# First expert of a fused attention and mixture-of-experts kernel: later issue of the loads of paired words, two pools for the converted weights, idle products moved ahead of the first gather

## The chip, the cores and the metric

One core of a Trainium2 chip runs the whole kernel as one program. The metric is the device time of that program in microseconds (us); less is better. Three runs of the kernel before gave 1026.57, 1030.37 and 1033.47 us; the median is 1030.37 us.

## The reference

The reference chains three parts. Causal attention with a learned position bias (4 batches, 8 heads, 576 tokens, 64 per head) gives a matrix x of 2304 tokens by 512. A first mixture of experts sends each token to one of 8 experts, 288 tokens to each, by a greedy assignment over sorted gate values, and applies two matrices with a ReLU between. A second block, the same for all tokens, applies `w_in` (512 by 2048), a mish-like function, and `w_out` (2048 by 512).

```
logits = x @ w_gate                      # greedy by value, 288 tokens to each expert
h = np.maximum(x[mask] @ w1[e], 0.0)     # e = 0..7, 512 -> 1024
out[mask] = h @ w2[e]                    # 1024 -> 512
...
h = x @ w_in                             # all tokens, 512 -> 2048
sp = np.log1p(np.exp(h))
return (h * np.tanh(sp)) @ w_out         # 2048 -> 512
```

## The kernel before, in words

**Split products.** All large products are made in a reduced-precision float type from split operands: each operand a has a high part (a copy rounded by ScalarE) and a low part (a minus the high part, by GpSimd for weights, by VectorE for activations). Every product is three matmuls (lines 497 to 499, `mm3`): high by high, high by low, low by high. A pass over one weight block is 12 matmuls of 128x288.

**Expert stages.** After attention, `experts` handles the experts one after the other. `route(e)` finds the 288 tokens of expert e (thresholds, counts, a list `idx`) and gathers their rows by three indirect DMAs issued by GpSimd (line 402, tile xg). `make_xt` turns the gathered rows by TensorE (line 531), ScalarE makes the high half (line 534) and VectorE the low half (line 535) of xu. `up(e)` runs the first mixture: for m = 0 to 7 a pass hp(m) = w1 block by xu, then act(m) (ScalarE line 558 for the high part, VectorE line 559 for the low part), and one step later a pass y(m-1) = w2 block by act(m-1). Its result goes to xu again (lines 578 and 579). `down(e)` runs the second block over 16 values of f: a pass with WI[f], the mish chain (lines 590 to 605), a pass with WO[f]. For expert 0, `route(0)` runs alone before `up(0)`; for the later ones route(e+1) is interleaved with up(e) and down(e).

**Weights.** Raw expert weights are loaded by SyncE's queue (line 458), copied to the high half by ScalarE (line 466), subtracted to the low half by GpSimd (line 467). In `up(0)` the sixteen blocks of the first expert are put into WI[8..15] and WO[8..15] (`home`), which `down(0)` needs later for the second block's own weights.

**Conversion of the second block's weights.** `w_in` and `w_out` come as 64-bit words that hold a double. The class `Convert` makes them into 32-bit floats and splits them, once, for all experts. Its units are 32 single ones (128x256) for WI[0..7], WO[0..7], and 16 paired ones (128x512) for WI[8..15], WO[8..15]. A unit is: a load into a buffer r2 (printed as r; three buffers, line 78; issued by ScalarE's queue in the expert stages), three VectorE operations (lines 115, 118, 121), then the split: a ScalarE copy (line 91) and a GpSimd subtraction (line 92). Some 21 single units are converted by VectorE during attention into the memory of xu, act and ot; they are held, and `settle` issues their splits during route(0). `run` is a generator: each `next` emits one VectorE operation (the third with the split), and the program calls it at fixed places (`conv`, `tick`). A paired unit may start only when `up(0)` has used the first expert's block in the same place (`gate`).

**What sets the order.** Every engine runs its instructions in the order in which the program emits them, and the order is the same in every run. ScalarE's queue carries its activations and also the loads of r2: an instruction that waits holds all that is behind it. In `run`, `fetch(i)` at the start of unit i issues the load of unit i+2. The buffer of that load was unit i-1's, so the load waits for the GpSimd subtraction of unit i-1.

**Pools.** All WI and WO tiles come from one pool, m_w, opened when attention's pools are closed; its memory is memory that attention's tiles used, and the first writers wait for the last users of those tiles, the stores of x to DRAM among them (lines 1075, 1078).

**Idle products.** `awake(n)` (line 679) issues n bf16 matmuls of 128x512 into a bank that nobody reads. Ahead of the first gather's data there are 18, and 4 more behind each third of `make_xt(0)`.

Of the kernel before, what the change touches and what calls it, by code (L numbers as in the profile page):

```python
# [30 lines left out]
def fb(ap):  # L31
    return ap.bitcast(F32)


class Convert:
# [25 lines left out]
        self.places = list(self.slots()) if self.wide else []  # L61
        self.limit = len(self.places)

    def grow(self, pool, stage, depth):
        for f in range(F2 // 128):
            self.WI.append(pool.tile([128, 2, DM // 128, 128], F32R, name=f"WI{f}"))
            self.WO.append(pool.tile([128, 2, DM], F32R, name=f"WO{f}"))
        self.limit, self.pool, self.depth, self.most = len(self.units), stage, depth, 4
# [10 lines left out]
        self.raw[self.loaded] = t  # L79
        self.loaded += 1  # L80

    def fetch(self, i):
        while self.loaded < min(self.limit, i + self.depth[0]):
            self.load()

    def split(self, unit, t):
# [11 lines left out]
    def run(self):  # L98
        nc = self.nc
        for i, unit in enumerate(self.units):  # L100
            while i >= min(self.limit, self.gate):
                yield
            self.fetch(i)
            t = self.raw.pop(i)
            keep = self.wide and i < len(self.places)
            if self.wide:
                w = t.bitcast(I32).rearrange("p c (f w) -> p c f w", w=2)
                if keep:
                    a = self.places[i]
                elif unit[3] == 1:  # L110
                    a = self.pool.tile([128, 2, 128], I32, name="c1", bufs=self.depth[1])
                else:
                    a = w[:, :, :, 1]
                b = a if self.temp is None else self.temp[:, :2 * unit[3]]
                nc.vector.tensor_scalar(b, w[:, :, :, 1], 3, 0x3FFFFFFF, op0=OP.logical_shift_left,
                                        op1=OP.bitwise_and)
                yield
                nc.vector.scalar_tensor_tensor(b, w[:, :, :, 1], -0x40000000, b, op0=OP.bitwise_and,
                                               op1=OP.bitwise_or)
                yield  # L120
                nc.vector.scalar_tensor_tensor(a, w[:, :, :, 0], 29, b, op0=OP.logical_shift_right,
                                               op1=OP.bitwise_or)
                t = fb(a)
                if keep:
                    self.held.append((unit, t))
            if not keep:
                self.split(unit, t)
            self.done += unit[3]
            yield
# [52 lines left out]
def build(ctx, tc, q, k, v, s, w_gate, w1, w2, w_in, w_out, out, debug=None):  # L182
# [29 lines left out]
    with ExitStack() as mctx:  # L212
        experts(mctx, tc, K, ring, ident, L, x_dram, w1, w2, cv, out)


def experts(ctx, tc, K, ring, ident, L, x_dram, w1, w2, cv, out):
    nc = tc.nc
    NF1, NF2, NC, NJ, JW = F // 128, F2 // 128, DM // 128, 3, CAP // 3
    rot = ctx.enter_context(tc.tile_pool(name="m_rot", bufs=2))
    one = ctx.enter_context(tc.tile_pool(name="m_one", bufs=1))  # L220
    W = ctx.enter_context(tc.tile_pool(name="m_w", bufs=1))
    ps_h = ctx.enter_context(tc.tile_pool(name="ps_h", bufs=1, space=PSUM))
    ps_y = ctx.enter_context(tc.tile_pool(name="ps_y", bufs=4, space=PSUM))
    ps_r = ctx.enter_context(tc.tile_pool(name="ps_r", bufs=1, space=PSUM))

    cv.grow(W, rot, (3, 4))
    cv.queue = nc.scalar
# [20 lines left out]
    def hbank():  # L248
        if cv.done == 4 * NF2 and len(free) == 2:
            free.insert(0, words)  # L250
        free.append(free.pop(0))
        return free[-1]
# [234 lines left out]
    def conv(n):  # L487
        for _ in range(n):
            next(cv.steps, None)
# [34 lines left out]
    def make_xt(e, parts=range(NJ), between=0):  # L524
        for j in parts:
            if j == 0:
                XT[e] = ring("xu", [128, 2, NC, CAP], F32R)
            xg, xt = R[e, "xg"][j], XT[e]
            p = hbank()
            for c in range(NC):  # L530
                nc.tensor.transpose(p[:, JW * c:JW * c + JW], xg[:JW, 128 * c:128 * c + 128], ident[:JW, :JW])
            src = p[:, :NC * JW].rearrange("p (c t) -> p c t", c=NC)
            js = slice(JW * j, JW * j + JW)
            nc.scalar.activation(xt[:, 0, :, js], src, AF.Copy)
            nc.vector.tensor_sub(xt[:, 1, :, js], src, fb(xt)[:, 0, :, js])  # L535
            if between:
                awake(between)
# [139 lines left out]
    def awake(n, at=None):  # L677
        for _ in range(n):
            nc.tensor.matmul(idle if at is None else at, upper, upper[:, None, :].to_broadcast([128, 4, 128]),
                             start=True, stop=True)  # L680
# [12 lines left out]
    cv.settle(99)  # L693
    rows(bank)
    conv(8)
    awake(18)
    make_xt(0, range(NJ), 4)
    conv(4)
    feed()
    for e in range(E):  # L700
# [503 lines left out]
```

## Time and profile before

| | us |
|---|---|
| median of three runs (lowest, highest) | 1030.37 (1026.57, 1033.47) |
| the profiled execution | 1027.31 |
| its span, first to last instruction | 1025.6 |
| mean granted TensorE clock, share of full speed | 0.984 |
| TensorE matmul busy | 957.2 (93%) |
| ScalarE busy | 631.8 (62%) |
| VectorE busy | 607.1 (59%) |
| GpSimd busy | 462.1 (45%) |

All rows below come from the one profiled execution. PE is TensorE's matmul, PEld its weight load, DVE VectorE, ACT ScalarE, POOL GpSimd, SP SyncE; ACTq is ScalarE's queue while it issues a DMA. In a timeline row the first number is the start in us from the start of the span, the second the duration in us; brackets hold the idle time of that engine just before and what ended it. Which instruction ended it is inferred, and where an engine stood behind a DMA in its own queue the name given can be another's. Attention ends at about 283 us, route(0) at 310, up(0) runs from 315 to 357, down(0) to 428, and the other seven experts take about 85 us each.

### The profile page before, as it was taken

What the parts mean: (1) busy time and instruction counts of PE and PEld (TensorE: products, weight loads), DVE (VectorE), ACT (ScalarE), POOL (GpSimd) and SP (SyncE); (2) the same over time, 40 slices, a digit from 0 to 9 for tenths busy, and PEclk for the clock granted to TensorE, in tenths of its full rate; (3) what the DMA queues carried; (4) which work ended last, traced back from release to release, by engine and by line L of the source; (5) the groups of instructions that cost most, each with busy time, mean ns of one, the idle gap of its engine ahead of it and who ended that gap; (6) DMA issues with size and microseconds to landing.
All of it is one profiled execution on the core that took longest, in us unless ns stands there. A gap on an engine that the chain in (4) does not pass through costs nothing.

```text
span 1025.6 us, 21405 instructions
## 1 busy us (share of the span) xinstructions
PE 957.2 (93%) x7679; PEld 901.2 (88%) x7679; DVE 607.1 (59%) x1871; ACT 631.8 (62%) x1403; POOL 462.1 (45%) x485
## 2 busy tenths in 40 slices
PE   5889998999988689899999999999999999999996
PEld 4779887888847588899999999999999999999996
DVE  6877898898586668446445544643644554343342
ACT  7668766777844366536745745663674575675563
POOL 2888888787677623360260343126026024502401
PEclk8999999999999899999999999999999999999998
DMA  5677686763147423231231121213123122401200
GB/s 123 159 173 169 162 213 158 177 163 88 44 141 246 130 66 114 65 95 47 61 106 42 56 76 41 66 53 96 42 66 106 36 62 77 135 12 38 69 1 24
DMA packets 131058, 97.31 MB, mean 95 GB/s; under 512 B 63272, under 2 KB 113608, under 8 KB 130920
## 3 DMA queue, kind: packets, MB, share of 16 engines
q1 hardware_dynamic: 120280, 75.24, 28.3%
q10 hardware_dynamic: 7600, 11.27, 3.5%
q0 software_dynamic: 3072, 9.44, 3.0%
q8 instruction: 60, 0.98, 0.4%
q14 instruction: 46, 0.38, 0.1%
HBM read 69.55 MB, written 9.73 MB: 77 GB/s over the span
## 4 chain that ended last, share of the span: by engine, by line
PE 60%; DVE 14%; issue 13%; ACT 6%; POOL 5%; DMA 1%; ACTq 0%; SPq 0%; POOLq 0%; DVEq 0%
PE y L497 8%; PE y L498 7%; PE y L499 7%; PE hp L497 5%; PE hp L498 5%; PE hp L499 5%; PE words L497 3%; PE words L499 2%; PE words L498 2%; PE rt L298 2%; PE t L935 2%; PE pv L1042 1%; PE pv L1040 1%; DVE junk L941 1%; PE s L1005 1%
## 5 line engine op out<-in xcount | busy, mean ns | idle before, releaser
L467 POOL TENSOR_TENSOR wt<-raw,wt 128x512 fp32r<-128x512 f32 x112 | 142.9, 1290 | 194.3 <-ACT wt L466 193.8
L497 PE MATMUL y<-act,WO 128*128 128x288 f32 x516 | 155.4, 301 | 3.3 <-ACT act L558 3.3
L1020 POOL TENSOR_TENSOR Pl<-P,Ph 128x384 fp32r<-128x384 f32 (+2 forms) x128 | 136.8, 1080 | 45.3 <-DVE Ph L1019 23.4
L498 PE MATMUL y<-act,WO 128*128 128x288 f32 x516 | 154.0, 298 | 0.2
L499 PE MATMUL y<-act,WO 128*128 128x288 f32 x516 | 153.0, 296 | 0.0
L497 PE MATMUL hp<-xu,WI 128*128 128x288 f32 x372 | 114.6, 308 | 6.7 <-DVE c L599 2.9
L498 PE MATMUL hp<-xu,WI 128*128 128x288 f32 x372 | 110.5, 297 | 0.2 <-DVE xu L535 0.2
L499 PE MATMUL hp<-xu,WI 128*128 128x288 f32 x372 | 110.1, 296 | 0.0
L497 PEld LDWEIGHTS y<-act,WO 128*128 128x128 f32 x516 | 98.0, 190 | 3.6 <-ACT act L558 3.5
L498 PEld LDWEIGHTS y<-act,WO 128*128 128x128 f32 x516 | 97.9, 190 | 0.8 <-DVE act L605 0.6
L499 PEld LDWEIGHTS y<-act,WO 128*128 128x128 f32 x516 | 97.7, 189 | 0.0
L402 POOL DMA_INDIRECT xg<-x_dram,idx x24 | 22.5, 939 | 162.2 <-DVE rt L408 156.8
L466 ACT ACTIVATE wt<-raw 128x512 fp32r<-128x512 f32 x112 | 70.0, 625 | 41.5 <-PE y L499 21.8
L599 DVE SCALAR_TENSOR_TENSOR hp<-c,hp 128x288 f32<-128x288 f32 x75 | 34.5, 460 | 87.8 <-ACT c L594 87.8
L591 ACT ACTIVATE c<-c 128x288 f32<-128x288 f32 x128 | 56.4, 440 | 44.9 <-DVE c L590 41.8
L1012 ACT ACTIVATE P<-s 128x384 f32<-128x384 f32 (+2 forms) x128 | 63.3, 503 | 30.2 <-PE s L1005 18.6
L497 PEld LDWEIGHTS hp<-xu,WI 128*128 128x128 f32 x372 | 70.9, 190 | 10.6 <-DVE c L599 4.5
L1040 PE MATMUL pv<-Ph,VH 128*128 128x320 f32 (+4 forms) x224 | 71.1, 318 | 3.5 <-DVE xT L1059 3.5
L498 PEld LDWEIGHTS hp<-xu,WI 128*128 128x128 f32 x372 | 70.7, 190 | 0.7 <-DVE xu L535 0.4
L499 PEld LDWEIGHTS hp<-xu,WI 128*128 128x128 f32 x372 | 70.7, 190 | 0.0
L1003 PE MATMUL s<-QKB 128*128 128x320 f32 (+4 forms) x224 | 69.4, 310 | 0.8 <-DVE mx L941 0.8
L497 PE MATMUL y<-act,wt 128*128 128x288 f32 x224 | 69.1, 309 | 0.0
(288 smaller groups left out, 2962.8 us busy)
## 6 DMA issues: line engine op xcount, KB each, us to landing
raw<-in_moe_w_dram SPq DMA_DIRECT2D x120, 256.0 KB
QKB<-qk SPq DMA_DIRECT2D x55, 288.0 KB
qkraw<-in_q_dram SPq DMA_DIRECT2D x32, 128.0 KB
qkraw<-in_k_dram SPq DMA_DIRECT2D x32, 128.0 KB
vraw<-in_v_dram SPq DMA_DIRECT2D x32, 128.0 KB
x_dram<-xn SPq DMA_DIRECT2D x16, 256.0 KB
r<-in_moe_w_in_dram ACTq DMA_DIRECT2D x8, 512.0 KB
r<-in_moe_w_out_dram ACTq DMA_DIRECT2D x8, 512.0 KB
```

Source lines behind the costliest of these rows:

```text
L402: nc.gpsimd.indirect_dma_start(out=xg[:JW], out_offset=None, in_=x_dram, in_offset=bass.IndirectOffsetOnAxis(ap=idx[:JW, j:j + 1], axis=0))
L466: nc.scalar.activation(t[:, 0], r, AF.Copy)
L467: nc.gpsimd.tensor_sub(t[:, 1], r, fb(t)[:, 0])
L497: nc.tensor.matmul(out_ap, ah, bh, start=first, stop=False)
L498: nc.tensor.matmul(out_ap, ah, bl, start=False, stop=False)
L499: nc.tensor.matmul(out_ap, al, bh, start=False, stop=last)
L591: nc.scalar.activation(a, a, AF.Exp)
L599: nc.vector.scalar_tensor_tensor(u, a, 0.5, p[:, :CAP], op0=OP.subtract, op1=OP.mult)
L1003: nc.tensor.matmul(p[:m, at:at + n], KB[i][:, h, kc], QB[i][:, h, q0:q1], start=ti in (1, 2) and j == 0, stop=False, skip_group_check=True)
L1012: nc.scalar.activation(P[:, :n], p[:, :n], AF.Exp, scale=0.125)
L1020: nc.gpsimd.tensor_sub(Pl[:, :n], P[:, :n], fb(Ph)[:, :n])
L1040: nc.tensor.matmul(o, VH[i][:, a, hs], ph, start=first, stop=False)
```

## The change

Three edits, all around the first expert. First, `fetch` gets an argument `less`; for paired units in the expert stages the load of unit i+2 is not issued at the start of unit i but behind its second VectorE operation. Second, the WI and WO tiles come from two pools, m_w0 for f = 0 to 7 and m_w1 for f = 8 to 15. Third, 24 instead of 18 idle products stand ahead of the first gather's data, and 2 instead of 4 behind each third of `make_xt(0)`: 30 in both kernels.

```
-    def grow(self, pool, stage, depth):
+    def grow(self, pools, stage, depth):
         for f in range(F2 // 128):
+            pool = pools[f // 8]
             self.WI.append(pool.tile([128, 2, DM // 128, 128], F32R, name=f"WI{f}"))
             self.WO.append(pool.tile([128, 2, DM], F32R, name=f"WO{f}"))
...
-    def fetch(self, i):
-        while self.loaded < min(self.limit, i + self.depth[0]):
+    def fetch(self, i, less=0):
+        while self.loaded < min(self.limit, i + self.depth[0] - less):
             self.load()
...
-            self.fetch(i)
+            late = self.most == 4 and unit[3] == 2
+            self.fetch(i, late)
             t = self.raw.pop(i)
...
                 nc.vector.scalar_tensor_tensor(b, w[:, :, :, 1], -0x40000000, b, op0=OP.bitwise_and,
                                                op1=OP.bitwise_or)
                 yield
+                self.fetch(i)
                 nc.vector.scalar_tensor_tensor(a, w[:, :, :, 0], 29, b, op0=OP.logical_shift_right,
                                                op1=OP.bitwise_or)
...
-    W = ctx.enter_context(tc.tile_pool(name="m_w", bufs=1))
+    W = [ctx.enter_context(tc.tile_pool(name=f"m_w{i}", bufs=1)) for i in range(2)]
...
-    awake(18)
-    make_xt(0, range(NJ), 4)
+    awake(24)
+    make_xt(0, range(NJ), 2)
```

The order of VectorE, GpSimd and SyncE stays as it was; on TensorE six idle products change places, on ScalarE 14 loads. In the pieces below the lines of the kernel after are 1 to 3 higher (L79 is L78 of before, L92 L91, L561 L558, L469 L466, L581 L578, L682 L679). ScalarE's queue at the end of up(0), kernel before: WI and WO with a number are weight tiles, r buffers of paired words, act<-hp the high part of act(m).

```order
L558 ACTIVATE act<-hp_4631 128x288 [waits PE_49]
L78 DMA r_5426<-in_moe_w_out_dram 128x512 [waits DMAHW3_49,Pool_49]
L466 ACTIVATE WO_4624<-raw 128x512
L91 ACTIVATE WO_4614<-r_5355 128x512 [waits DMAHW1_49,DVE_49]
L78 DMA r_5472<-in_moe_w_in_dram 128x4x128 [waits Pool_49]
L558 ACTIVATE act<-hp_4630 128x288 [waits PE_49]
L91 ACTIVATE WI_4615<-r_5396 128x512 [waits DMAHW2_49,DVE_49]
L78 DMA r_5507<-in_moe_w_out_dram 128x512 [waits Pool_49]
L578 ACTIVATE xu<-y 128x288 [waits PE_49] x4
L91 ACTIVATE WO_4616<-r_5426 128x512 [waits DMAHW3_49,DVE_49]
```

The same stretch of ScalarE's queue in the kernel after.

```order
L561 ACTIVATE act<-hp_4634 128x288 [waits PE_49]
L469 ACTIVATE WO_4627<-raw 128x512
L79 DMA r_5464<-in_moe_w_out_dram 128x512 [waits Pool_49]
L92 ACTIVATE WO_4617<-r_5386 128x512 [waits DMAHW1_49,DVE_49]
L561 ACTIVATE act<-hp_4633 128x288 [waits PE_49]
L79 DMA r_5493<-in_moe_w_in_dram 128x4x128 [waits Pool_49]
L92 ACTIVATE WI_4618<-r_5415 128x512 [waits DMAHW2_49,DVE_49]
L581 ACTIVATE xu<-y 128x288 [waits PE_49] x4
L79 DMA r_5543<-in_moe_w_out_dram 128x512 [waits Pool_49]
L92 ACTIVATE WO_4619<-r_5464 128x512 [waits DMAHW3_49,DVE_49]
```

Before, the load that waits for GpSimd stands ahead of act(7) and another ahead of xu; after, act(7) and xu stand ahead of them, and each load stands right ahead of the line-92 copy of its own unit.

ScalarE's queue at the end of attention, kernel before: the first copy of a held unit into WI[0], and what it waits for.

```order
L78 DMA r_4643<-in_moe_w_out_dram 128x256
L91 ACTIVATE WI_4593<-xu 128x256 [waits DMAHW6_49,DMAHW5_49,DMAHW7_49,DMAHW0_49,Pool_49]
L91 ACTIVATE WI_4593<-xu 128x256
L91 ACTIVATE WO_4594<-xu 128x256 x2
```

The same place in the kernel after.

```order
L79 DMA r_4646<-in_moe_w_out_dram 128x256
L92 ACTIVATE WI_4596<-xu 128x256 x2
L92 ACTIVATE WO_4597<-xu 128x256 x2
```

The wait of the first copy for four queues of DMAs and for GpSimd is gone; nothing changes places.

## Rows read from the trace of the kernel before

**Rows 1.** The page, part 2: TensorE's busy tenths in 40 slices.
```profile
PE   5889998999988689899999999999999999999996
```

**Rows 2.** Windows: us, busy (instructions) of PE, PEld, DVE, ACT, POOL; PEclk, DMA share, GB/s.
```profile
315.30:357.30 42.00, 32.54 (x233) 28.73 (x231) 28.55 (x67) 16.16 (x33) 27.81 (x25) 0.93 0.54 165
...
427.70:512.00 84.30, 83.96 (x726) 81.92 (x725) 42.23 (x135) 49.30 (x112) 26.10 (x25) 1.00 0.22 65
...
310.20:313.30 3.10, 3.09 (x13) 2.05 (x14) 0.56 (x1) 0.49 (x1) 3.10 (x4) 0.50 0.99 301
...
351.20:361.30 10.10, 7.52 (x27) 6.76 (x28) 6.50 (x15) 3.07 (x7) 1.98 (x3) 0.50 0.33 104
...
341.00:345.00 4.00, 3.47 (x32) 2.59 (x32) 3.13 (x5) 1.55 (x4) 3.19 (x3) 1.00 0.29 112
```

**Rows 3.** Waits of TensorE in 315.3 to 357.3: us in total, times, longest.
```profile
PE y L497 <- ACT act L558: 5.9, 4, 3.3
```

**Rows 4.** Timeline, end of up(0), several engines.
```profile
341.05 0.40 PE L497 MATMUL y<-act,WI 128*128 128x288 f32 x1 [1.50 <-ACT act L558]
...
350.29 1.28 POOL L92 TENSOR_TENSOR WO<-r,WO 128x512 fp32r<-128x512 f32 x1
351.61 0.39 ACTq L78 DMA_DIRECT2D r<-in_moe_w_in_dram  x1
352.04 0.41 ACT L558 ACTIVATE act<-hp 128x288 fp32r<-128x288 f32 x1 [2.49 <-POOL WO L92]
...
352.50 0.61 PE L497 MATMUL y<-act,WO 128*128 128x288 f32 x1 [3.31 <-ACT act L558]
...
357.29 0.61 PE L497 MATMUL hp<-xu,WI 128*128 128x288 f32 x1 [1.28 <-ACT xu L578]
```

**Rows 5.** Timeline, route(0) to the start of up(0); last row: landing times of the gathers.
```profile
284.26 1.06 ACTq L78 DMA_DIRECT2D r<-in_moe_w_out_dram  x2
287.50 0.72 ACT L91 ACTIVATE WI<-xu 128x256 fp32r<-128x256 f32 x2 [3.25 <-DMA r<-in_moe_w_out_dram]
...
287.99 1.42 POOL L92 TENSOR_TENSOR WI<-xu,WI 128x256 fp32r<-128x256 f32 x2 [5.31 <-DMA r<-in_moe_w_in_dram]
...
303.71 0.16 DVE L396 TENSOR_REDUCE idx<-rt 96x3 int32<-96x6 f32 x1 [0.52 <-PE rt L382]
...
305.48 1.13 POOL L402 DMA_INDIRECT xg<-x_dram,idx  x1 [0.19 <-DVE words L118]
...
308.15 0.92 POOL L402 DMA_INDIRECT xg<-x_dram,idx  x1 [0.30 <-issue]
...
303.54 4.04 PE L679 MATMUL y<-upper 128*128 128x512 bf16 x18
310.21 0.90 PE L531 MATMUL hp<-ident,xg 96*128 96x96 f32 x4 [2.63 <-DMA xg<-x_dram,idx]
...
315.33 0.42 PE L497 MATMUL hp<-xu,WI 128*128 128x288 f32 x1
...
DMA to landing us min/median/max: 4.6/4.7/4.7
```

**Rows 6.** Timeline, up(0): first and last link of a chain on GpSimd, and a VectorE operation of a paired unit.
```profile
329.85 1.30 POOL L92 TENSOR_TENSOR WI<-r,WI 128x512 fp32r<-128x512 f32 x1 [1.87 <-ACT WI L91]
...
349.06 1.26 POOL L467 TENSOR_TENSOR WO<-raw,WO 128x512 fp32r<-128x512 f32 x1 [1.12 <-ACT WO L466]
...
328.33 0.69 DVE L121 SCALAR_TENSOR_TENSOR r<-r,words 128x512 int32<-128x512 int32 x1
```

**Rows 7.** Timeline: the load of paired words for WI[11], and its first use.
```profile
344.22 0.39 ACTq L78 DMA_DIRECT2D r<-in_moe_w_in_dram  x1
...
348.79 0.69 DVE L115 TENSOR_SCALAR words<-r 128x512 int32<-128x512 int32 x1
```

**Rows 8.** Timeline, down(0): a load in ScalarE's queue and the activation behind it.
```profile
378.79 0.39 ACTq L78 DMA_DIRECT2D r<-in_moe_w_in_dram  x1
379.22 0.45 ACT L591 ACTIVATE c<-c 128x288 f32<-128x288 f32 x1 [1.41 <-DVE words L118]
```

## The prediction, made before the result was known

> **What bounds the kernel now.** I read the page's slices first: TensorE is at 8 or 9 tenths nearly everywhere [rows 1], so time can only be had where it waits or runs slowly. The windows by stage then say where: from expert 1 on it is busy for 83.96 of 84.30 us, while in up(0) it is busy for 32.54 of 42.00 us and part of that at a lower clock [rows 2]. So the stretch to study is route(0), up(0) and down(0), and the seven later experts will move as a block. In the waits of up(0) the largest entry is y waiting for act: 5.9 us in four waits, the longest 3.3 [rows 3].
>
> The timeline shows what such a wait is made of [rows 4]. GpSimd's subtraction for WO[10] runs from 350.29 to 351.57. At 351.61, right behind it, ScalarE's queue issues a load, which had to wait for that subtraction since the two use the same buffer. act(7) stands behind the load and starts at 352.04, though its input had been ready for some us, and y starts at 352.50 after 3.31 us of idle time. TensorE's granted clock is then 0.50 (1.2 instead of 2.4 GHz) from 351.2 to 361.3 [rows 2]. It also fell after the 2.63 us idle ahead of the first gather: 0.50 from 310.2 to 313.3 [rows 2, 5]. After an idle time of 1.50 us it did not fall: 1.00 in 341 to 345 [rows 2, 4].
>
> **The change part by part.** I work against the profiled execution, 1027.31 us (its span is 1025.6, so 1.7 lie outside).
>
> *Two pools.* ScalarE has issued its loads by 284.26 + 1.06 = 285.32, but its first copy of a held unit starts at 287.50, after 3.25 us idle [rows 5]. The order shows what goes: its waits for four DMA queues and GpSimd. That is 2.1 us. GpSimd's subtractions follow ScalarE, and run from 287.99 without a gap until the gather at 305.48, which had only 0.19 us of idle time ahead of it; its list, idx, was there at 303.71 + 0.16 = 303.87 [rows 5]. So GpSimd, not the route, holds the gather, and with a start 2.1 us earlier it is free at 303.2 and the gather starts behind idx, at 304.05: 1.4 us earlier. The third gather goes from 308.15 to 306.7.
>
> *Idle products.* 18 take 4.04 us [rows 5], so 24 take 5.39: from 303.54 to 308.93. All three gathers land 4.6 to 4.7 us after issue [rows 5]; the first then lands at 308.7, the third at 311.35. The idle time of 2.63 us vanishes, and with it, by the pattern above, the fall of the clock. The last four turns take about 0.5 us at full clock, as much as ScalarE's copy behind them, so up(0) starts at 311.4 + 0.5 + 0.5 = 312.4 instead of 315.33. **Term 1: -2.9 us.** Products behind the turns cost nothing, since the landings are later than they. If the gather stays at 305.48, the third lands at 312.75 and up(0) starts at 313.8: -1.5. If the gathers share the DMA engines with the raw loads more than before (DMA share 0.99 in this stretch, [rows 2]) and land 1 us later, -1.9.
>
> *Later loads, in up(0).* The first pair's conversion ends on VectorE at 329.02 [rows 6]. What leads to it follows the start of up(0) and loads that run at full DMA share, so I let it move by 2.6 rather than 2.9: 326.4. From there GpSimd has 12 subtractions up to that of WO[15]: five of pairs, seven of the expert's own blocks. Before, they took from 329.85 to 349.06 + 1.26 = 350.32, 20.5 us [rows 6]; at 1.28 us each they are 15.4 us of work. The other 5.1 us are waits for ScalarE, which stood behind its loads, and for VectorE, which stood behind act. After the change the copies of the expert's blocks no longer stand behind the load that waits for the pair in progress, but only behind one that waits for the pair before. Going through the three queues by hand, with 0.7 us for each VectorE operation and ScalarE copy, I find two waits left, 1.0 us ahead of WO[8] and 1.3 us ahead of WO[9], where VectorE's three conversions are the longer way. So the chain lasts 17.7 us, from 326.4 + 0.7 = 327.1 to 344.8. The last y needs that block and 12 matmuls: it ends at 347.0. Before it ended at 357.29 - 1.28 = 356.0 [rows 4]. That is 9.0 us, of which 2.9 is term 1. **Term 2: -6.1 us**, in which 1.7 us are the last y at full instead of half clock. By this walk the longest wait of TensorE left in up(0) is 1.5 us, as long as the one after which the clock stayed. Bounds: with no waits in the chain it is -8.4; if the chain keeps all its 5.1 us of waits and only act comes in time, -3.3, or -1.6 if the clock falls all the same.
>
> *The start of down(0).* xu no longer waits for the load behind WI[11], but the copy of WI[11] itself still stands ahead of xu, so I leave that wait (1.28 us) as it is. TensorE ran at half clock from 357.29 to 361.3 [rows 2, 4]: 4.0 us of work that would take 2.0, of which the low halves of xu keep a part. **Term 3: -1.5 us** (bounds 0 and -2.0).
>
> *Later loads, in down(0).* A load at 378.79 holds ScalarE, whose next operation starts after 1.41 us of idle time [rows 8]; the name in brackets is VectorE's, but the load ends its wait just there. Behind the second operation of its unit the load finds GpSimd long done. VectorE's mish steps follow. I take half: **term 4: -0.7 us** (bounds 0 and -1.4).
>
> *What the later issue costs.* The place costs no instruction; the lead of each load gets shorter. In my walk the tightest is WI[11]: issued near 339.8, first used near 343.8, a lead of 4.0 us. Before, the same load was issued at 344.22 and used at 348.79, without a wait on VectorE's part, so 4.57 us is an upper bound of its landing [rows 7]. Two loads late by up to 0.57 us are 0 to 1.1 us; I take **0.7 us, term 5**. In down(0) one unit lasts longer and no lead is short.
>
> Here stands a rule of the Trainium skill that speaks against the change: the page "DMA: Bandwidth & Descriptors", section "Rules for kernel authors", advises to issue a DMA early and to wait late, so that its fixed cost lies beside other work. The trace shows the price of the early place: the issuing queue is itself the wait [rows 4]. By the rule alone terms 2 to 4 would be losses, and that is the slower rival below.
>
> **The sum.** -2.9 - 6.1 - 1.5 - 0.7 + 0.7 = -10.5 us: 1016.8 against the profiled execution. The median of the three runs lies 3.1 us above that execution, so the same gain from there gives 1019.9. I predict 1018.5, in the middle.
>
> **The rivals.**
> *The chain keeps its waits.* GpSimd's idle time in up(0) comes from VectorE and the landing of the raw blocks as much as from the loads. For it: I found by hand only two of its waits, and ScalarE still stands behind a load that waits for GpSimd, one unit earlier. Then -2.9 for the start, -3.3 + 1.7 = -1.6 with the clock falling, -0.5 for down: -5, about 1024.
> *The gather does not move.* The row of the first gather names a VectorE operation as what released it, not GpSimd [rows 5]. If its wait counts that operation, term 1 is -1.5 and all else follows: -9, about 1020. Against it: that operation neither writes idx nor reads what the gather reads.
> *More than forecast.* The chain runs without waits: 2.3 us more, and no late load: -13.5, about 1015.
> *Late loads starve the conversion: slower.* A load is issued behind the second operation of unit i and used by unit i+2, so two units can't take less than its landing plus the three operations of 0.7 us. Eight pairs belong to up(0) and the start of down(0); before, one came every 4.1 us (20.5 us for five). With a landing L the period is (L + 2.1) / 2; eight periods eat the 3.6 us of terms 1 and 4 when L is (4.1 + 0.45) x 2 - 2.1 = 7.0 us. From there on it is slower: at 8 us by 8 x 0.95 - 3.6 = 4 us, about 1033. Against it: 4.57 us bounds the landing of one such load, and gathers at full DMA share took 4.7 [rows 5, 7].
>
> **How the numbers follow.** Forecast 0.50, chain keeps its waits 0.25, gather does not move 0.10, more than forecast 0.10, late loads 0.05. A measurement of this kernel can tell about 1% from no change, 10.3 us. The forecast and its neighbours lie close to that edge, seen from the median: the prediction is 1.15% below it. I count most of the forecast case, part of the unmoved gather and all of "more" as faster by over 1%: 0.55. The rest of these and the kept waits are within 1%: 0.41. The late loads need a landing that no row comes near to: 0.04. The range reaches from a little below "more than forecast" with the lower basis, 1010, to 1028, where the kept waits with the upper basis end; it leaves out the late loads and little else.
>
> **What would show it right or wrong.** Right: the first copy into WI[0] starts near 285.4, the first gather near 304.0, up(0) near 312.4, with the granted clock at 1.00 in between; waits of y for act in up(0) fall from 5.9 us to 2 or less, no idle time of TensorE there is over 1.5 us, and no stretch at clock 0.50 lies between 310 and 400; the later experts take what they took. Wrong: VectorE's first operations of pairs wait for loads of r, or act still starts right behind a load; GpSimd's 12 subtractions take 20 us again; or the clock falls after a wait of 1.5 us.

## The result and the profile after

| | before | changed kernel |
|---|---|---|
| median, us | 1030.22 (6 runs) | 1020.04 (6 runs, 1019.03 to 1025.04) |
| ratio of the runs, 95% interval | | 0.9915 (0.9894 to 0.9936) |
| profiled execution, us | 1027.31 | 1020.92 |
| its span, us | 1025.6 | 1019.2 |

A ratio of 0.9915 is 8.8 us of 1030. The forecast was 1018.5 us with a gain of 10.5; the time lies in the range, and the gain is just under the 1% that I set as the edge, which lies inside the interval. So the case within 1%, to which I had given 0.41 against 0.55 for more, came by less than the interval can tell. A second set gave 0.9915 again (the fifth run below).

The two profiled executions can't be laid over each other by the clock on the wall: attention, which the change doesn't touch, ended at another time in each. I therefore count from one ScalarE row at its end, which writes `bits`. First that row in the timeline of the kernel before, with a row of its down(0) that has not been shown yet (time, duration, engine, line, operation, tiles, count, and in brackets the idle time ahead and what ended it).

```profile
283.94 0.31 ACT L266 ACTIVATE bits<-weight 128x128 bf16<-128x128 f32 x1
...
411.54 0.40 PE L497 MATMUL words<-xu,WI 128*128 128x288 f32 x1 [2.36 <-DVE r L121]
```

The same two rows of the changed kernel:

```profile
285.21 0.31 ACT L269 ACTIVATE bits<-weight 128x128 bf16<-128x128 f32 x1
...
405.07 0.40 PE L500 MATMUL words<-xu,WI 128*128 128x288 f32 x1 [2.36 <-DVE r L124]
```

So everything in the changed kernel's profile stands 1.27 us later on the wall, and a row that moved by x on the wall moved by x - 1.27 against its own start. "Behind the anchor" below means less 283.94 or 285.21. The spans end 741.7 and 734.0 us behind it: -7.7.

The windows by stage (columns as in [rows 2]; the first line is the whole of up(0)) answer to [rows 2].

```profile
314.57:351.70 37.13, 30.92 (x231) 27.52 (x231) 28.05 (x66) 15.60 (x33) 27.50 (x26) 1.00 0.62 192
427.70:512.00 84.30, 84.08 (x712) 82.10 (x711) 41.88 (x134) 49.59 (x113) 25.98 (x25) 1.00 0.22 63
310.20:313.30 3.10, 1.62 (x12) 0.98 (x12) 0.45 (x1) 1.49 (x4) 3.10 (x4) 1.00 1.03 249
351.20:361.30 10.10, 6.29 (x54) 5.41 (x54) 6.39 (x16) 5.88 (x15) 2.60 (x2) 1.00 0.32 101
```

up(0) takes 37.1 us instead of 42.0, the later experts are as full as before, and the granted clock is 1.00 in both stretches where it was 0.50. TensorE's slices on the page, which [rows 1] show of before, change in one place: the fourteenth, which holds most of the end of up(0), rises from 6 to 8 tenths. No other digit moves by more than one; the whole gain is less than half a slice.

```profile
PE   5889998998988888899999999999999999999996
```

The waits of TensorE in up(0), which answer to [rows 3]: y's wait for act falls from 5.9 us to 1.6.

```profile
PE y L500 <- ACT act L561: 1.6, 3, 0.6
...
PE hp L500 <- ACT xu L581: 0.7, 1, 0.7
```

The timeline of the end of up(0), which answers to [rows 4]:

```profile
345.98 1.33 POOL L93 TENSOR_TENSOR WI<-r,WI 128x512 fp32r<-128x512 f32 x1
...
346.96 0.69 DVE L124 SCALAR_TENSOR_TENSOR r<-r,words 128x512 int32<-128x512 int32 x1
...
347.26 1.30 POOL L470 TENSOR_TENSOR WO<-raw,WO 128x512 fp32r<-128x512 f32 x1
347.34 0.33 ACTq L79 DMA_DIRECT2D r<-in_moe_w_out_dram  x1
347.78 0.67 ACT L92 ACTIVATE WO<-r 128x512 fp32r<-128x512 f32 x1 [2.22 <-DVE r L124]
348.35 0.39 ACT L561 ACTIVATE act<-hp 128x288 fp32r<-128x288 f32 x1
348.53 1.30 POOL L93 TENSOR_TENSOR WO<-r,WO 128x512 fp32r<-128x512 f32 x1
...
348.80 0.40 PE L500 MATMUL y<-act,WO 128*128 128x288 f32 x1 [0.65 <-ACT act L561]
...
351.68 0.40 PE L500 MATMUL hp<-xu,WI 128*128 128x288 f32 x1 [0.66 <-ACT xu L581]
```

In [rows 4] act started right behind a load that had waited for the subtraction of the pair in progress. Here act starts at 348.35, before that subtraction (348.53) has begun. The load at 347.34 still waits: it starts right behind the subtraction of the pair before (345.98 + 1.33 = 347.31). But the first thing behind it is the copy of its own pair, whose conversion on VectorE ends just as late (346.96 + 0.69 = 347.65), so this wait costs next to nothing. The expert's own subtraction at 347.26, last of the twelve, is no longer held up either.

The front, which answers to [rows 5]:

```profile
286.63 0.72 ACT L92 ACTIVATE WI<-xu 128x256 fp32r<-128x256 f32 x2 [1.12 <-issue]
...
304.98 0.16 DVE L399 TENSOR_REDUCE idx<-rt 96x3 int32<-96x6 f32 x1 [0.52 <-PE rt L385]
...
305.43 1.14 POOL L405 DMA_INDIRECT xg<-x_dram,idx  x1 [1.08 <-DMA raw<-in_moe_w_dram]
...
304.80 5.34 PE L682 MATMUL y<-upper 128*128 128x512 bf16 x24
311.68 0.55 PE L534 MATMUL hp<-ident,xg 96*128 96x96 f32 x4 [1.54 <-DMA xg<-x_dram,idx]
...
314.60 0.40 PE L500 MATMUL hp<-xu,WI 128*128 128x288 f32 x1
```

ScalarE's first copy comes 2.14 us earlier behind the anchor, and the gather 1.32 us earlier: it now follows idx by 0.3 us, with 1.08 us of idle time on GpSimd ahead of it. But the first turn comes 6.25 us after the gather's issue instead of 4.7, so up(0) gains 2.0 us, not 2.9.

VectorE's waits for words in up(0), its conversion of the first pair, and GpSimd's first paired subtraction, which answer to [rows 6], with the next two of GpSimd's twelve subtractions that had to wait:

```profile
315.62 0.43 DVE L117 TENSOR_SCALAR words<-r 128x256 int32<-128x256 int32 x1 [0.49 <-DMA r<-in_moe_w_in_dram]
...
317.46 0.43 DVE L117 TENSOR_SCALAR words<-r 128x256 int32<-128x256 int32 x1 [0.42 <-DMA r<-in_moe_w_in_dram]
...
321.64 0.43 DVE L117 TENSOR_SCALAR words<-r 128x256 int32<-128x256 int32 x1 [2.08 <-DMA r<-in_moe_w_out_dram]
...
323.72 0.43 DVE L117 TENSOR_SCALAR words<-r 128x256 int32<-128x256 int32 x1 [0.43 <-DMA r<-in_moe_w_out_dram]
...
329.69 0.69 DVE L124 SCALAR_TENSOR_TENSOR r<-r,words 128x512 int32<-128x512 int32 x1
...
331.20 1.30 POOL L93 TENSOR_TENSOR WI<-r,WI 128x512 fp32r<-128x512 f32 x1 [1.89 <-ACT WI L92]
...
334.80 1.31 POOL L93 TENSOR_TENSOR WO<-r,WO 128x512 fp32r<-128x512 f32 x1 [1.05 <-issue]
...
342.23 1.32 POOL L93 TENSOR_TENSOR WO<-r,WO 128x512 fp32r<-128x512 f32 x1 [1.11 <-ACT WO L92]
```

VectorE's waits for loads of r in up(0) of the kernel before (us in total, times, longest):

```profile
DVE words L115 <- DMA r<-in_moe_w_out_dram: 1.8, 2, 1.0
```

Here the 2.0 us are gone: the first paired subtraction starts 45.99 us behind the anchor, 45.91 before. Most of what up(0) gained at its start VectorE lost in four waits for loads of r, 3.4 us in all (1.8 in two before). The twelve subtractions then take 331.20 to 347.26 + 1.30 = 348.56, 17.4 us instead of 20.5.

The start of down(0), timeline of TensorE; first two rows of the kernel before:

```profile
363.73 0.40 PE L497 MATMUL hp<-xu,WI 128*128 128x288 f32 x1 [0.33 <-DVE c L599]
367.08 0.41 PE L497 MATMUL hp<-xu,WI 128*128 128x288 f32 x1 [1.50 <-DVE c L599]
```

The same two of the changed kernel:

```profile
357.99 0.40 PE L500 MATMUL hp<-xu,WI 128*128 128x288 f32 x1 [1.39 <-DVE c L602]
361.35 0.40 PE L500 MATMUL hp<-xu,WI 128*128 128x288 f32 x1 [1.50 <-DVE c L602]
```

Full clock there only brings TensorE earlier to a wait for VectorE's mish steps.

### The profile page after: what moved, and what is told of

It reads as the page before. It is cut to its first block, busy times and chain, and to the rows that moved or that the text cites. A ratio compares the mean times of both kernels' runs of the same rounds, so it can differ in the third digit from the quotient of the medians.

```text
span 1019.2 us, 21406 instructions
## 1 busy us (share of the span) xinstructions
PE 953.9 (94%) x7679; PEld 898.0 (88%) x7679; DVE 606.6 (60%) x1871; ACT 631.5 (62%) x1403; POOL 462.2 (45%) x485
## 4 chain that ended last, share of the span: by engine, by line
PE 48%; issue 6%; DVE 2%; POOL 1%; ACT 1%; DMA 1%; POOLq 0%; ACTq 0%
PE y L500 8%; PE y L501 8%; PE y L502 7%; PE hp L500 5%; PE hp L501 5%; PE hp L502 5%; PE words L500 3%; PE words L502 2%; PE words L501 2%; PE rt L301 2%; PE hp L663 1%; POOL wt L470 1%; DVE mask L293 1%; PE hp L534 0%; PE rt L385 0%
## 5 line engine op out<-in xcount | busy, mean ns | idle before, releaser
L469 ACT ACTIVATE wt<-raw 128x512 fp32r<-128x512 f32 x112 | 70.0, 625 | 44.0 <-PE y L502 18.9
L500 PEld LDWEIGHTS hp<-xu,WI 128*128 128x128 f32 x372 | 70.1, 188 | 10.9 <-DVE c L602 5.6
L501 PEld LDWEIGHTS hp<-xu,WI 128*128 128x128 f32 x372 | 70.0, 188 | 1.4 <-DVE xu L582 1.0
L502 PEld LDWEIGHTS hp<-xu,WI 128*128 128x128 f32 x372 | 70.0, 188 | 0.0
```

Source lines behind the costliest of these rows:

```text
L469: nc.scalar.activation(t[:, 0], r, AF.Copy)
L500: nc.tensor.matmul(out_ap, ah, bh, start=first, stop=False)
L501: nc.tensor.matmul(out_ap, ah, bl, start=False, stop=False)
L502: nc.tensor.matmul(out_ap, al, bh, start=False, stop=last)
```

## The experiments

Theory 1: the late loads make nearly all of the gain; the pools and the idle products move the start of up(0), and the loads, which keep the DMA engines full from 304 to 326 (share 1.03 here, 0.98 before), take it back by the first pair. Theory 2: each part brings its gain where it stands. Theory 3: late loads starve the conversion. The share is that of the sixteen DMA engines' time, by a count that can pass 1; the two windows of 304 to 326, the changed kernel first:

```profile
304.00:326.00 22.00, 19.73 (x134) 14.58 (x133) 13.08 (x35) 9.88 (x23) 16.40 (x18) 1.00 1.03 308
...
304.00:326.00 22.00, 19.19 (x118) 14.81 (x117) 13.49 (x37) 10.88 (x24) 18.49 (x21) 0.92 0.98 299
```

Each set of four shared its runs of the kernel before (medians 1028.85, 1028.6 and 1028.36).

| kernel | median us | ratio (95%) | up(0) starts | first paired subtraction | twelve subtractions | longest wait of y for act | down(0) starts | span ends |
|---|---|---|---|---|---|---|---|---|
| before | | | 31.39 | 45.91 | 20.5 | 3.3 | 73.35 | 741.7 |
| changed | 1020.04 | 0.9915 (0.9894, 0.9936) | 29.39 | 45.99 | 17.4 | 0.65 | 66.47 | 734.0 |
| 1 late loads only | 1021.82 | 0.9942 (0.9930, 0.9955) | 30.65 | 45.95 | 17.4 | 0.65 | 66.42 | 732.8 |
| 2 pools only | 1028.57 | 1.0001 (0.9990, 1.0011) | 31.34 | 46.44 | 20.5 | 3.3 | 73.88 | 742.1 |
| 3 idle products only | 1028.4 | 1.0007 (0.9996, 1.0018) | 31.11 | 46.49 | 20.5 | 3.2 | 73.93 | 742.5 |
| 4 pools and idle products | 1029.0 | 1.0005 (0.9991, 1.0018) | 29.41 | 45.89 | 20.5 | 3.3 | 73.34 | 742.0 |
| 8 before, loads of r from SyncE | 1023.86 | 0.9954 (0.9938, 0.9970) | 29.30 | 52.62 | 17.4 | 6.1 | 72.74 | 738.5 |
| 9 changed, four blocks later | 1017.84 | 0.9889 (0.9874, 0.9905) | 30.85 | 44.91 | 17.6 | 0.6 | 65.59 | 732.7 |

Starts and the end of the span are us behind the anchor row of each profile (one execution each; the changed kernel's second profile, of run 5, ends at 733.3); the twelve and the waits are us.

**Runs 1 to 4: one part alone.** Run 1 is the first edit below (with the new argument of `fetch` from the change), run 2 the one of the pools, run 3 the one of the idle products, run 4 the last two together.

```diff
+            late = self.most == 4 and unit[3] == 2
-            self.fetch(i)
+            self.fetch(i, late)
...
+                self.fetch(i)
```
```diff
+            pool = pools[f // 8]
...
-    W = ctx.enter_context(tc.tile_pool(name="m_w", bufs=1))
+    W = [ctx.enter_context(tc.tile_pool(name=f"m_w{i}", bufs=1)) for i in range(2)]
```
```diff
-    awake(18)
-    make_xt(0, range(NJ), 4)
+    awake(24)
+    make_xt(0, range(NJ), 2)
```

> The first expert's paired loads issued behind the unit's second operation, and nothing else of the change. Theory 1 (late loads make nearly all of it; pools and idle products change nothing while the DMA engines are full until about 326): 1022 to 1024 us; the twelve GpSimd subtractions take about 17.5 us instead of 20.5, no wait of y for act over 1.5 us in the first up stage, the granted clock at 1.00 in 351 to 361, but at 0.50 at the first gather as before. Theory 2 (each part brings its gain where it stands, the front 2 us of it): 1024 to 1026. Theory 3 (late loads starve the conversion): 1030 or more.

> The two pools and nothing else of the change. Theory 1: 1029 to 1031 us (same): ScalarE's first copy of the first expert about 2 us earlier, the first pair's conversion on VectorE within 0.5 us of where it was, the twelve subtractions still 20.5 us, the clock at 0.50 in 351 to 361. Theory 2: 1028 to 1029, the first pair 1 to 2 us earlier.

> Six more idle products and the transposes two products earlier, and nothing else of the change. Theory 1: 1029 to 1031 us (same): the clock stays at 1.00 in 310 to 313, but the first wait for paired words in up ends where it did. Theory 2: 1028 to 1029.5.

> The pools and the idle products together, the loads where they were: all of the change but the late loads. Theory 1: 1029 to 1031 us (same): up begins about 2 us earlier and gives that back at its first paired words, whose conversion on VectorE starts within 0.7 us of 329; the long wait of y for act (3.3 us in before) stays above 2.5. Theory 2: 1026.5 to 1028, the first pair's conversion about 2 us earlier.

But for two details told below, the rows of theory 1 came in all four, the first pair of runs 2 and 3 at the edge (0.5 us later than before). The times of runs 1 to 3 lay just under its ranges, and those of runs 2 and 3 inside theory 2's. But the kernel before took 1028.85 in this set, and by their ratios runs 2 to 4 gained nothing; nor did their first pair come earlier by the 1 to 2 us of theory 2. Theory 3 fell with run 1. Of the late loads alone, the timeline of GpSimd's first and last of the twelve:

```profile
329.42 1.30 POOL L92 TENSOR_TENSOR WI<-r,WI 128x512 fp32r<-128x512 f32 x1 [1.89 <-ACT WI L91]
...
345.49 1.30 POOL L469 TENSOR_TENSOR WO<-raw,WO 128x512 fp32r<-128x512 f32 x1
```

The window of the same kernel at its first gather:

```profile
310.20:314.00 3.80, 3.59 (x23) 2.13 (x24) 1.12 (x2) 1.41 (x3) 3.80 (x4) 1.00 1.06 309
```

Of the pools and idle products together, the first and last of the twelve and the long wait of y in the timeline:

```profile
330.00 1.31 POOL L93 TENSOR_TENSOR WI<-r,WI 128x512 fp32r<-128x512 f32 x1 [1.89 <-ACT WI L92]
...
349.21 1.27 POOL L468 TENSOR_TENSOR WO<-raw,WO 128x512 fp32r<-128x512 f32 x1 [1.12 <-ACT WO L467]
...
352.65 0.61 PE L498 MATMUL y<-act,WO 128*128 128x288 f32 x1 [3.31 <-ACT act L559]
```

Either of the two parts alone hardly moves the start of up(0) (31.34 and 31.11 against 31.39). In run 4 it comes 2.0 us earlier, as in the changed kernel, and nothing of it is left at the first pair (45.89) or at down(0) (73.34). The two details of the expectations that missed: in run 3 the clock did fall at the first gather (0.50 in 312 to 315, after 2.34 us of idle time), and in run 1 it did not (the window above, after 3.21 us), but was at 0.83 in 351.2 to 361.3, where I had written 1.00.

**Run 5: the changed kernel again.** Its ratio had come out below that of run 1, so it was run beside runs 6 to 8.

> The changed kernel as it is, beside the next three. Theory 1 (the pools and the idle products add nothing even with the late loads): 1020 to 1023 us, ratio to before 0.992 to 0.996, as for the late loads alone. Theory 2 (they add 2 us once the late loads are there): 1018.5 to 1020.5, ratio 0.989 to 0.992.

1020.13 us, 0.9915 (0.9895 to 0.9935): the case of theory 2. That the rest was worth 2 us beside late loads stayed open until runs 10 to 12.

**Run 6: four blocks loaded later (the edit moved nothing).**

```diff
-        return n < 3 * NRAW + min(at["split"], NRAW) + max(0, at["split"] - 3 * NRAW)
+        return n < 3 * NRAW + min(max(0, at["split"] - 4), NRAW) + max(0, at["split"] - 3 * NRAW)
```

> The changed kernel with the last four of the second expert's blocks (256 KB each, those that SyncE issues at 314) loaded four conversions later. If the DMA engines, full from 304 to 326, are what pins the first pair's conversion: 1 MB less at some 310 GB/s is up to 3 us less in that stretch, VectorE's waits for r (3.4 us in the changed kernel) fall under 1.5, the first subtraction of a pair on GpSimd starts 1 to 2 us earlier, and the kernel takes 1017.5 to 1019.5 us. Rival, VectorE's own row of work pins it: no change, 1020 to 1021. Second rival: the four blocks come late for their own conversions on ScalarE, 1021 to 1023.

1019.25 us, 0.9908 (0.9888 to 0.9928), first pair at 45.76. The four are the last of the first expert's own sixteen blocks, not the second expert's, as the expectations of this run and of runs 7 to 9 have it: the list of loads begins with the sixteen of the first expert, and SyncE issues 4, 8 and 4 up to here. SyncE's queue shows why the run tells nothing of them:

```profile
312.29 4.60 SPq L461 DMA_DIRECT2D raw<-in_moe_w_dram  x4
```

That is 28.45 us behind the anchor, 28.76 in the changed kernel. Their later place in the program did not hold these loads back: SyncE's queue had nothing else to wait for.

**Run 7: four instead of six blocks ahead of the gather.**

```diff
-    at = {"load": 0, "split": 0, "use": 0, "early": 6}
+    at = {"load": 0, "split": 0, "use": 0, "early": 4}
```

> The changed kernel with four instead of six of the second expert's blocks loaded ahead of the gather. If what stands in the DMA engines ahead of the gather is what made its landing 6.2 us instead of 4.7: the landing takes about 5 us, the up stage starts 1 us earlier, the rest of the loads end no earlier, and the kernel takes 1019.5 to 1021 us (no change, since the first pair stays pinned). Rival (the start of up counts): 1018.5 to 1019.5.

1019.26 us, 0.9912 (0.9892 to 0.9933). The first turn finds its rows there, the gather having been issued at 304.70:

```profile
309.24 0.50 PE L534 MATMUL hp<-ident,xg 96*128 96x96 f32 x4
```

So the blocks ahead of the gather had made its landing 6.25 us long; here it took at most 4.54. up(0) starts 28.46 us behind the anchor, 0.9 earlier, and the first paired subtraction 45.66, 0.3 earlier. The time lies in the rival's range, but beside run 5 (0.9915) the ratio shows no difference, and the span ends 733.2 us behind the anchor, against 734.0 and 733.3 for the changed kernel. That most of the earlier start is lost by the first pair is what theory 1 says; the time can't decide it.

**Run 8: the kernel before, all its loads of r in the expert stages from SyncE.**

```diff
-    cv.queue = nc.scalar
```

> The kernel before with the first expert's loads issued by SyncE instead of ScalarE, as early in the program as they were. If the harm was that a load waiting for its buffer stops ScalarE's copies behind it: the twelve GpSimd subtractions take about 17.5 us, y waits for act under 1.5 us, and it takes 1021 to 1025 us with no lead given up. Rival (the order in which the buffers come free, not the engine that waits, sets the chain): 20.5 us for the twelve, 1028 to 1031. Second rival: SyncE's own loads of the second expert stand behind the waiting ones, and the first wait moves there: 1026 to 1034.

The cause of the gain stands apart here, since no load was moved later in the program. SyncE's queue, VectorE, TensorE, and GpSimd's first and last of the twelve:

```profile
316.20 6.36 SPq L78 DMA_DIRECT2D r<-in_moe_w_out_dram  x2
...
320.78 0.43 DVE L115 TENSOR_SCALAR words<-r 128x256 int32<-128x256 int32 x1 [7.23 <-DMA r<-in_moe_w_in_dram]
...
323.04 0.61 PE L496 MATMUL y<-act,WI 128*128 128x288 f32 x1 [6.12 <-ACT act L557]
...
336.33 1.31 POOL L92 TENSOR_TENSOR WI<-r,WI 128x512 fp32r<-128x512 f32 x1 [1.87 <-ACT WI L91]
...
352.45 1.29 POOL L466 TENSOR_TENSOR WO<-raw,WO 128x512 fp32r<-128x512 f32 x1
```

The waits for buffers now stand in SyncE's queue (two loads over 6.36 us), and the twelve subtractions take 17.4 us as with late loads: it was the load in ScalarE's queue that stretched them. The second rival held too, with the first expert's own blocks: SyncE issues these until 314.7, the loads of r stand behind them, VectorE waits 7.23 us once and TensorE 6.12, and the first pair is 6.7 us late. That the later start itself shortens the twelve, this run can't exclude; in the others their length doesn't follow it (17.3 to 17.6 us with late loads for starts of 44.9 to 47.2, 20.5 without for 45.9 to 46.5). The sum is still 0.9954.

The Trainium skill's page "DMA: Bandwidth & Descriptors", section "Rules for kernel authors", advises to issue early and wait late. [rows 4] show what the early issue costs where the issuing engine has work of its own behind the load, and run 8, as early in the program but from another queue, does not have that cost on ScalarE. That the early issue saves time no run here shows: the late loads of the changed kernel kept no operation of VectorE waiting from the first pair on.

**Run 9: four blocks truly later.**

```diff
-        return n < 3 * NRAW + min(at["split"], NRAW) + max(0, at["split"] - 3 * NRAW)
+        return n < 3 * NRAW + min(max(0, at["split"] - 7), NRAW) + max(0, at["split"] - 3 * NRAW)
...
             t = rot.tile([128, NC, 128], F32, name="raw", bufs=NRAW)
+        if n == 3 * NRAW:
+            nc.gpsimd.memset(t[0:1, 0, 0:1], 0.0)
```

> The changed kernel, where the last four of the second expert's blocks (1 MB) now truly stand back: the first of them is written to by GpSimd behind its eighth conversion of that expert, so that SyncE issues it at about 327 instead of 314 (the run with the loads four conversions later left them at 312.3 and tells nothing of them). If the DMA engines, full from 304 to 326, pin the first pair's conversion: VectorE's waits for r (3.4 us) fall under 2 and the first paired subtraction on GpSimd comes 1 to 2 us earlier than 46.0 us after the row that casts bits; 1018 to 1019.5 us. Rival, VectorE's row and the issue of the loads pin it: 45.7 to 46.5 us as in every run so far, no change in time, 1019 to 1021. Second rival: the four blocks come late for their conversions near 340, 1021 to 1024.

SyncE's queue, VectorE's only wait for r, and GpSimd's first pair (anchor at 289.02):

```profile
331.23 2.15 SPq L463 DMA_DIRECT2D raw<-in_moe_w_dram  x4
...
324.28 0.43 DVE L117 TENSOR_SCALAR words<-r 128x256 int32<-128x256 int32 x1 [0.77 <-DMA r<-in_moe_w_out_dram]
...
333.93 1.30 POOL L93 TENSOR_TENSOR WI<-r,WI 128x512 fp32r<-128x512 f32 x1 [1.48 <-ACT WI L92]
```

With 1 MB less ahead of it the first pair comes 1.1 us earlier than in the changed kernel, although up(0) itself started 1.5 us later, with the clock down at the gather. VectorE's waits for r fall from 3.4 to 0.8 us, so the loads that stood ahead of it had held the pair. What is left, VectorE's own row of conversions and routing, was not tried. Its median is the lowest of all, 1017.84 us, just under its range. But its interval overlaps those of the changed kernel and of runs 10 to 12, and its span ends 732.7 us behind the anchor, as that of run 1 (732.8): a gain over these is not shown.

**Runs 10 to 12: late loads alone, with the idle products, with the pools.** Their edits are those of runs 1 to 3.

> The late loads alone once more, beside the next two, since its ratio (0.9942, 0.9930 to 0.9955) and that of the whole change (0.9915 twice, 0.9895 to 0.9935) hardly overlap. Theory 1 (nothing else counts): 0.992 to 0.994. Theory 2 (pools and idle products are worth some 2 us once the loads are late): 0.9935 to 0.9955.

> The late loads with the idle products, without the two pools. Theory 1: as late loads alone. Theory 2, if what is gained is the clock at the first gather and behind it: some 1 us better than late loads alone (ratio 0.992 to 0.9935), the clock at 1.00 in 310 to 316.

> The late loads with the two pools, without the six idle products. Theory 1: as late loads alone. Theory 2, if what is gained is the earlier start on ScalarE and at the gather: some 1 us better than late loads alone (ratio 0.992 to 0.9935).

1020.33, 1019.68 and 1019.49 us; 0.9910 (0.9897 to 0.9924), 0.9910 (0.9897 to 0.9924) and 0.9907 (0.9893 to 0.9921). Side by side the late loads alone do as much as with either of the other parts; the whole change, 0.9915, was not in this set. Run 10's ratio lies under both its ranges; in that runs 11 and 12 are as run 10, theory 1 holds. Why the same kernel had 0.9942 in run 1, with an interval that doesn't reach this one, stays open; its profiled execution there, 1018.03 us, was the fastest of its seven. The profiles show nothing of it behind the anchor: the span ends there at 732.8 us in run 1 and 733.3 in run 10, at 734.2 and 734.0 in runs 11 and 12. Of the 5.6 us between the profiled executions of runs 1 and 10 (1018.03 and 1023.67), 5.1 lie ahead of the anchor. Run 10 also says most about the front: its up(0) started 33.26 us behind the anchor, 3.9 later than in the changed kernel, and the span ended no later. So 0.3% between sets is not to be read as a part's worth, and up to that much of the other two parts beside the late loads can't be excluded.

## Why the prediction was right, and where it was not

What failed is the step "so I let it move by 2.6 rather than 2.9". Its reason, loads at full DMA share, was in the same sentence, and I drew too little from it: the first pair moved by +0.1 us. Term by term, behind the anchor:

- **Term 1, forecast -2.9: 0 by the first pair.** First copy -2.14 (forecast -2.1) and gather -1.32 (-1.4) were right. The landing grew to 6.25 us, where my bound had 1 us more; run 7 shows that blocks ahead of the gather did it. up(0) started 2.0 us earlier, and runs 4, 7, 9 and 10 show where that went: no trace shows any of it at the end of the span, to within the 0.7 us by which the two profiles of the changed kernel differ.
- **Term 2, forecast -6.1: -6.3.** The mechanism and the chain were right: 17.4 us (forecast 17.7), with the two waits that I had found by hand (1.05 and 1.11 us, forecast 1.0 and 1.3), and the longest wait of y for act 0.65. The loads wait for the pair before, as I wrote. The last y ends 65.81 us behind the anchor (351.68 - 0.66 - 285.21) against 72.07. Of the -9.0 that I expected there with term 1, 2.7 are missing, which is what the front was to bring to the first paired subtraction.
- **The start of down(0).** I left xu's wait at 1.28; it is 0.66, -0.6 not forecast. **Term 3, forecast -1.5: -0.1.** The second mish wait ends 76.14 us behind the anchor against 83.14 (367.08 before), -7.0, after -6.9 at the start of the stage: TensorE at full clock waits 1.39 us where at half clock it waited 0.33. My bound of 0 was the nearer one.
- **Term 4, forecast -0.7: -0.7.** In down(0) each late load starts 1.9 us or more behind the last subtraction, as I expected; no run separates this term from the rest. The products of words start 119.86 us behind the anchor against 127.60, -7.7.
- **Term 5, forecast +0.7: 0.** From the first pair on no operation of VectorE in up(0) or down(0) waits for a load of r. The rival of late loads had no ground.

The sum is -7.7, which the spans confirm, instead of -10.5. The ratio says 8.8, and the two medians lie 10.2 apart: that the time came so close to 1018.5 owes as much to the basis as to the sum, and that part is luck. Of the rivals, "the chain keeps its waits" fell by the 17.4 us, and "the gather does not move" by the 1.32. Of the signs that I named, the first copy, the waits of y, the clock and the later experts came as forecast; up(0) near 312.4 and the gather near 304.0 are to be read with 1.27 us added, and up(0) missed by 0.9.

## What to carry to other kernels

A load that waits for its buffer is an instruction of the engine that issues it: put it behind whatever that engine owes to others, or on an engine that owes nothing. Before you count a stage's earlier start, look for what the same stage is full of, here DMA from 304 to 326: a gain ahead of a full resource is taken back behind it. To find out what a change of three parts is worth, run each part alone and the likeliest one twice, beside the whole.

## What the runs showed that I had not expected

- The length of TensorE's last wait did not decide whether the granted clock fell from 1.00 to 0.50. It stayed after 3.21 us at the gather (run 1) and fell after 2.34 (run 3) and 3.27 (run 10). The wait of 2.36 us for words in down(0) was followed by 1.00 in the changed kernel and by 0.50 (404 to 406) in run 6, whose edit moved nothing there. My rule, read from two falls and one stay, was too simple; what else decides it stays open.
- The end of attention, which no kernel here changes, came between 283.47 and 289.02 us in the profiled executions: more than the whole effect of two of the three parts. Without a row as anchor the term by term account would have been noise.
